# Expert 0's tokens in a fused attention and two-MoE kernel: rows fetched beside the last chunk, the last chunk's own tokens placed by a 0/1 matrix

## The chip, the core and the metric

The kernel runs on one core of a Trainium2 chip. TensorE (PE) multiplies matrices, VectorE (DVE) and ScalarE (ACT) work elementwise on its results, GpSimd (POOL) works elementwise between tiles in SBUF and issues indirect DMAs, SyncE (SP) issues the other DMAs. Every engine works through its own queue in order. The metric is the time of one execution in microseconds, the median of several runs; beside it stands one execution taken with the profiler.

## The reference

What is computed, cut to what matters here:

```python
def _moe2_ref(x, w_gate, w1, w2):           # x: 2176 tokens x 512
    logits = x @ w_gate                      # 8 experts
    order = np.argsort(-logits.flatten())    # best (token, expert) pairs first
    assigned = -np.ones(N); counts = np.zeros(E)
    for idx in order:
        tok, e = idx // E, idx % E
        if assigned[tok] >= 0 or counts[e] >= cap:   # cap = 2176 / 8 = 272
            continue
        assigned[tok] = e; counts[e] += 1
    for e in range(E):
        mask = assigned == e
        out[mask] = np.maximum(x[mask] @ w1[e], 0.0) @ w2[e]

def reference(...):
    x = attention(q_l, k_l, v_l, q_g, k_g, v_g)      # local windows and global rows
    x = (relu(x @ w_in) + alpha * min(x @ w_in, 0)) @ w_out     # d_ff = 2048
    return _moe2_ref(x, w_gate, w1, w2)              # d_ff = 1024 per expert
```

Every expert ends with exactly 272 tokens, in an order of its own that depends on the data.

## The kernel before

Matrices are multiplied in two halves: a number is split into a high half (fp32r, made by ScalarE's cast) and a low half (the rest, by `split`, lines 70 to 73), and a product is the sum of high by high, low by high and high by low, three matmuls. Tokens go in 8 chunks of 272 (`CH`), columns of d_model in four quarters of 128 (`KD`).

The first MoE's second product for all chunks is done at the end of its stage, by `gemm2b` (L1178): for a chunk, 8 blocks `f` of the hidden size by four quarters by 3 are 96 matmuls (L1195), their weights the second half of `w_out`. Two quarters at a time accumulate in two PSUM banks (pool `pH` for the first two quarters, `p4` for the others), and VectorE adds them to the partial result `xo` (L1200). After a chunk its rows are turned by transposes (`rows`, L247), copied by ScalarE, and written to `x2d` in DRAM, one row per token; 16 leftover tokens of seven chunks are collected and written together (`tails`). These steps wait in a list `post` and are done among the next chunk's matmuls. The last chunk's own rows are turned by `last_blocks` (L267) and written by `last_out`.

Meanwhile a router (`phase`, `listing`) finds the experts one after the other on VectorE, with small matmuls on TensorE (counts `pc` L907, column sums `pa` L919, positions `pq`, lists `pl`, `ps`). Its generator is advanced by `advance(x)`, by as many microseconds of TensorE's planned work as the main loop has yielded. TensorE's order is the order in which the code is written (`manual_schedule`), so its router matmuls wait in its queue for VectorE, with the main matmuls behind them. The other engines' order is set by a scheduler from its own estimates.

After the last chunk, `fetch_x(0)` gathers the rows of expert 0's 272 tokens from `x2d` with three indirect DMAs of GpSimd (L1018), `gather(0)` turns them (L1054) and splits them into `xsh` and `xsl`, and `slot(k)` does an expert: `up` 8 x 12 matmuls (L1068), `down` 4 x 24 (L1084). The gather can start only when all rows of `x2d` are written, since an expert's tokens may lie anywhere. While TensorE has nothing else to do it runs 36 matmuls of ones (`busy`, tile `idle`, L108). The weights of expert k+1 come in 8 tiles of 128x1024 (`fetch_1`, `fetch_2`): a DMA into one of three raw buffers, ScalarE's cast, GpSimd's low half, 2.4 us of GpSimd each. PSUM pools have one bank (`px`, tag `tx`) or two (`pH`, `p4`, `pm`).

## Time and profile before

| | us |
|---|---|
| median of 3 runs (840.07 to 842.46) | 841.01 |
| the profiled execution | 843.68 |
| its span, first to last instruction | 841.7 |
| TensorE busy in it | 808.9 (96%) |
| VectorE, ScalarE, GpSimd busy | 473.6, 389.0, 347.9 |
| granted TensorE clock, mean | 0.989 |

Times in rows are microseconds from the span's start. Attention and the first MoE fill 0 to 475, the last products of the first MoE 475 to 591, the eight experts 604 to 832. A row of the timeline gives start, duration, engine, line, operation, out<-in and the number of instructions that it merges; of merged matmuls the duration holds the drain of the last. A bracket gives the idle time of the engine before the row and what ended it, as far as the trace shows; where "issue" or an engine long done is named, it was a wait that the trace doesn't show, often a DMA.

### The profile page before, as it was taken

What the parts mean: (1) busy time and instruction counts of PE and PEld (TensorE: products, weight loads), DVE (VectorE), ACT (ScalarE), POOL (GpSimd) and SP (SyncE); (2) the same over time, 40 slices, a digit from 0 to 9 for tenths busy, and PEclk for the clock granted to TensorE, in tenths of its full rate; (3) what the DMA queues carried; (4) which work ended last, traced back from release to release, by engine and by line L of the source; (5) the groups of instructions that cost most, each with busy time, mean ns of one, the idle gap of its engine ahead of it and who ended that gap; (6) DMA issues with size and microseconds to landing.
All of it is one profiled execution on the core that took longest, in us unless ns stands there. A gap on an engine that the chain in (4) does not pass through costs nothing.

```text
span 841.7 us, 21041 instructions
## 1 busy us (share of the span) xinstructions
PE 808.9 (96%) x8380; PEld 745.1 (89%) x8380; DVE 473.6 (56%) x1672; ACT 389.0 (46%) x970; POOL 347.9 (41%) x299
## 2 busy tenths in 40 slices
PE   6989999999998999999999999999899999999995
PEld 4767878888998999999898999999599999989995
DVE  5888975454389742254343257776577777652120
ACT  5785656465445643433232334341355545454421
POOL 1123413020136532320000365762499978779601
PEclk9989999999999999999999999999999999999998
DMA  9974733631145412011221216434266665656201
GB/s 343 380 287 125 276 120 108 225 129 49 33 167 179 139 52 81 21 60 55 76 84 55 80 53 193 139 77 138 81 219 209 202 194 162 188 164 202 102 26 38
DMA packets 47993, 115.99 MB, mean 138 GB/s; under 512 B 4183, under 2 KB 20951, under 8 KB 45847
## 3 DMA queue, kind: packets, MB, share of 16 engines
q1 hardware_dynamic: 44999, 105.73, 38.8%
q0 software_dynamic: 2896, 8.92, 3.1%
q8 instruction: 66, 1.08, 0.5%
q14 instruction: 32, 0.26, 0.1%
HBM read 96.80 MB, written 17.83 MB: 136 GB/s over the span
## 4 chain that ended last, share of the span: by engine, by line
PE 53%; issue 7%; POOL 4%; DVE 3%; DMA 2%; ACT 1%; POOLq 0%; DVEq 0%
PE h L192 16%; PE h L1195 12%; PE h L1084 7%; PE h L1068 6%; PE y L226 5%; POOL m L73 3%; PE lp L284 2%; DMA raw<-in_moe_w_dram 2%; PE pc L907 1%; PE xt L1054 1%; PE idle L108 1%; PE wp L142 1%; PE yt L247 1%; POOL xg L1018 1%; POOL out_dram L1118 1%
## 5 line engine op out<-in xcount | busy, mean ns | idle before, releaser
L192 PE MATMUL h<-xh,win 128*128 128x272 f32 x768 | 164.7, 300 | 2.9 <-ACT win L72 1.1
L73 POOL TENSOR_TENSOR m<-raw,m 128x1024 fp32r<-128x1024 f32 x64 | 152.1, 2401 | 12.8 <-ACT m L72 10.5
L192 PEld LDWEIGHTS h<-xh,win 128*128 128x128 f32 x768 | 126.7, 192 | 12.5 <-issue 5.0
L192 PE MATMUL h<-xl,win 128*128 128x272 f32 x384 | 112.5, 294 | 1.8 <-DVE xl L73 1.8
L73 POOL TENSOR_TENSOR glo<-g,ghi 128x272 fp32r<-128x272 f32 x64 | 54.6, 859 | 141.2 <-ACT ghi L72 139.6
L226 PE MATMUL y<-ghi,wout 128*128 128x272 f32 x512 | 109.2, 298 | 1.5 <-ACT wout L72 1.5
L1195 PE MATMUL h<-gr,wout 128*128 128x272 f32 x768 | 108.5, 294 | 0.0
L1068 PE MATMUL h<-xsh,m 128*128 128x272 f32 x512 | 105.0, 295 | 0.3 <-ACT xsh L72 0.3
L1084 PE MATMUL h<-hh,m 128*128 128x272 f32 x512 | 103.9, 294 | 0.0
L73 POOL TENSOR_TENSOR gr<-gb,gr 128x272 fp32r<-128x272 f32 x64 | 48.1, 783 | 131.2 <-ACT gr L72 130.7
L1195 PEld LDWEIGHTS h<-gr,wout 128*128 128x128 f32 x768 | 99.4, 189 | 0.5 <-ACT gr L72 0.4
L226 PEld LDWEIGHTS y<-ghi,wout 128*128 128x128 f32 x512 | 82.9, 188 | 6.8 <-issue 3.6
L197 ACT ACTIVATE neg<-h 128x272 f32<-128x272 f32 x128 | 49.9, 395 | 83.3 <-PE h L192 82.3
L1068 PEld LDWEIGHTS h<-xsh,m 128*128 128x128 f32 x512 | 82.1, 188 | 0.5 <-ACT xsh L72 0.5
L1084 PEld LDWEIGHTS h<-hh,m 128*128 128x128 f32 x512 | 81.6, 188 | 0.0
L72 ACT CAST m<-raw 128x1024 fp32r<-128x1024 f32 x64 | 65.5, 1048 | 34.8 <-DMA raw<-in_moe_w_dram 34.8
L192 PEld LDWEIGHTS h<-xl,win 128*128 128x128 f32 x384 | 73.6, 192 | 2.5 <-DVE xl L73 2.5
L1084 PE MATMUL h<-hl,m 128*128 128x272 f32 x256 | 75.2, 294 | 0.0
L1068 PE MATMUL h<-xsl,m 128*128 128x272 f32 x256 | 74.6, 291 | 0.0
L226 PE MATMUL y<-glo,wout 128*128 128x272 f32 x256 | 73.4, 290 | 1.0 <-POOL glo L73 1.0
L198 DVE SCALAR_TENSOR_TENSOR gb<-neg,al,h 128x272 f32<-128x272 f32 x64 | 31.5, 494 | 70.0 <-ACT neg L197 64.8
L400 ACT ACTIVATE pr<-sc,mx 128x128 f32<-128x128 f32 x128 | 49.9, 392 | 31.8 <-DVE mx L398 31.8
(233 smaller groups left out, 1522.8 us busy)
## 6 DMA issues: line engine op xcount, KB each, us to landing
raw<-in_moe_w_dram SPq DMA_DIRECT2D x64, 512.0 KB, 3.7
vv<-in_v_dram SPq DMA_DIRECT2D x16, 1024.0 KB, 8.4
qk<-in_qk_dram SPq DMA_DIRECT2D x14, 720.0 KB, 8.5
raw<-in_moe_w_in_dram SPq DMA_DIRECT2D x16, 512.0 KB, 4.7
raw<-in_moe_w_out_dram SPq DMA_DIRECT2D x16, 512.0 KB, 3.6
xs<-xb SPq DMA_DIRECT2D x16, 272.0 KB, 8.7
xpart<-xd SPq DMA_DIRECT2D x32, 136.0 KB, 2.5
xb<-xs SPq DMA_DIRECT2D x8, 544.0 KB, 3.9
```

Of the source, the lines that this page charges most:

```text
L72: a = A.copy(hi, src)
L73: return a, (lo_eng or V).tensor_tensor(lo, src, hi.bitcast(F32), op=OP.subtract)
L108: T.matmul(ps, x, x.unsqueeze(1).to_broadcast([128, 4, 128]), start=True, stop=True)
L192: T.matmul(ps, wi[:, w, k, fs], x[:, k], start=i == 0, stop=i == 3 * KD - 1)
L197: A.activation(out=neg, in_=ps, func=AF.Relu, scale=-1.0)
L198: epi[0] = V.scalar_tensor_tensor(g, neg, al1[:, hf * KH + f:hf * KH + f + 1], ps, op0=OP.mult, op1=OP.add)
L226: T.matmul(ps, wo[:, w, f, ds_], x[:, f], start=f == 0 and i == 0, stop=f == KH - 1 and i == 2)
L284: T.matmul(lp[r:r + 32], w, x, start=n < 4, stop=n >= LT - 4)
L400: A.activation(out=d["pr", j][:, ii], in_=sc, func=AF.Exp, bias=d["mx", j][:, ii:ii + 1], scale=-1.0, accum_out=d["sm", j][:, ii:ii + 1])
L1068: T.matmul(ps, d["w1"][:, w, kk, fs], x[:, kk], start=i == 0, stop=i == 3 * KD - 1)
L1084: T.matmul(ps, d["w2"][:, w, f, ms], x[:, f], start=i == 0, stop=i == 3 * K3 - 1)
L1195: T.matmul(ps[j], wo[:, w, f, ds_], x, start=f == 0 and a == 0, stop=f == KH - 1 and a == 2)
```

## The change

For the last chunk `gemm2b` is replaced by `last`. It takes the quarters one after the other, each in one bank of `p4` (before: the first two side by side in `pH`). After each quarter `turn` transposes its three token blocks, ScalarE copies them for the write to `x2d`, and they are split (`yh`/`yl` or `yhl`), the low half on GpSimd for the first three quarters. Expert 0's list is clipped (`IDE`): a token of the last chunk is replaced by row 1904, the last chunk's first row, which is written as zeros early on and overwritten only after the fetch. So `fetch_x(0)` needs only the other chunks' rows and is issued during the last chunk; `others` transposes what it brought and copies it to `xe`. The last chunk's own tokens are placed by a matmul: `late_oh`, a 0/1 matrix of 272 tokens by 272 slots, made by VectorE (`late_lists`) right after expert 0's list, from positions that three small DMAs have moved to the chunk's rows (`late_slots`). `take` does the 6 matmuls of a quarter (three token blocks, high and low half), VectorE adds `xe`, ScalarE makes the high and GpSimd (for the last quarter VectorE) the low half.

Expert 0's `up` starts with two blocks at once in `p4`: the 12 products that need only the high halves of the first three quarters, then their 6 with the low half, then the last quarter. The fillers (`busy`) are gone. Cut to what the steps need:

```diff
+        def late_slots(pos):
+            V.tensor_scalar(late_at, pos[:, c14:], -1.0, None, op0=OP.add)
+            V.memset(late_pos, -1.0)
+            nc.sync.dma_start(out=late_pos[:128 - OFF, :2], in_=late_at[OFF:, :2])
...
+        def late_lists():
+            V.tensor_scalar(IDE, IDS[:, 0], float(NTOK - CH), None, op0=OP.min)
+            for b in range(NL):
+                for q, (a, e) in enumerate(blk):
+                    V.tensor_scalar(late_oh[0][:, b, a:e], fr[:, :e - a], late_pos[:, b:b + 1], float(-a),
+                                    op0=OP.subtract, op1=OP.is_equal)
...
         def fetch_x(k):
-            xg = sl.tile([128, 3, DM], F32, name="xg")
+            ids = IDS[:, k] if k else IDE
+            xg = sx.tile([128, 3, DM], F32, name="xg")
             for q, (a, b) in enumerate(SEG):
-                st = P.indirect_dma_start(out=xg[:b - a, q], out_offset=None, in_=x2d,
-                                          in_offset=bass.IndirectOffsetOnAxis(ap=IDS[:b - a, k, q:q + 1], axis=0))
+                P.indirect_dma_start(out=xg[:b - a, q], out_offset=None, in_=x2d if k else x2d[:NTOK - CH + 1],
+                                     in_offset=bass.IndirectOffsetOnAxis(ap=ids[:b - a, q:q + 1], axis=0))
...
+            if k == 0:
+                yield from up(k, (0, 1), range(KD - 1), (0, 2))
+                yield from up(k, (0, 1), range(KD - 1), (1,))
+                yield from up(k, (0, 1), (KD - 1,))
+                f = 2
...
+        def last():
...
+            def turn(d):
+                t = px.tile([128, NL, 128], F32, name="yt", tag="tx")
+                for b, a in enumerate((0, 128, CH - 128)):
+                    T.transpose(t[:, b], xo[:, d, a:a + 128], ident)
...
+                r = gx2.tile([128, NL, 128], F32, name="yr", tag="yr", bufs=3)
+                if d < KD - 1:
+                    A.copy(r, t)
+                    split(*hl, r, lo_eng=P)
+                else:
+                    split(*hl, t)
+                    A.copy(r, t)
...
+            def others(q):
...
+                t = pH.tile([128, KD, 128], F32, name="xt", tag="h1")
+                for d in range(KD):
+                    T.transpose(t[:, d, :n], SLOT[0]["xg"][:n, q, d * 128:(d + 1) * 128], ident[:n, :n])
+                A.copy(SLOT[0]["e"][:, :, a:b], t[:, :, :n])
...
+            def take(d):
+                t = pH.tile([128, CAP], F32, name="xt", tag="h1")
+                for i, hl in enumerate(rows_hl[d]):
+                    for b in range(NL):
+                        T.matmul(t, hl[:, b], late_oh[0][:, b], start=i == 0 and b == 0, stop=i == 1 and b == NL - 1)
+                xh, xl = SLOT[0]["x"]
+                x = SLOT[0]["e"][:, d]
+                V.tensor_tensor(x, t, x, op=OP.add)
+                SLOT[0]["cast"] = split(xh[:, d], xl[:, d], x, lo_eng=P if d < KD - 1 else V)[0]
...
+                    if d == 0 and f and post:
+                        post.pop(0)()
+                        yield 0.4
+                        if not post:
+                            fetch_x(0)
+                    if d and f == 3:
+                        turn(d - 1)
+                        yield 0.4
+                    if d == KD - 1 and f > 4:
+                        others(f - 5)
+                        yield 0.4
+                V.tensor_tensor(xo[:, d], ps, xo[:, d], op=OP.add)
+            for d in range(KD):
+                take(d)
+                if d == 0:
+                    turn(KD - 1)
...
-        st = fetch_x(0)
-        idle = p4.tile([128, 4, 128], F32, name="idle", tag="h4")
-        for _ in range(NB0):
-            busy(idle, ones, 2)
-            advance(0.43)
-        for x in gather(0):
-            busy(idle, ones, 4)
-            advance(x + 0.9)
```

TensorE's order at the end of the last chunk, before (`h` is a main product, `yt` the chunk's own rows turned, `idle` the fillers; behind these rows come more fillers, router counts, the 12 transposes `xt` and then expert 0's first product):

```order
L1195 MATMUL h_8369<-gr,wout 128x272 x15
L267 MATMUL yt<-ident,pt 128x128 x6
L267 MATMUL yt<-ident,pt 16x128 x3
L1195 MATMUL h_8369<-gr,wout 128x272 x9
L267 MATMUL yt<-ident,pt 128x128 x2
L267 MATMUL yt<-ident,pt 16x128
L108 LDWEIGHTS ones
L108 MATMUL idle<-ones 128x512
```

The same place after, from the last three main products on (`xt<-late_oh` is a placement, `h<-xsh` and `h<-xsl` expert 0's products with the high and the low half, `pa` a router sum):

```order
L1289 MATMUL h_8475<-gr,wout 128x272 x3
L1270 MATMUL xt<-ident,xg 128x16 x4
L1277 MATMUL xt<-late_oh,yhl 128x272 x6
L1243 MATMUL yt<-ident,pt 128x128 x3
L1277 MATMUL xt<-late_oh,yh 128x272 x3
L1277 MATMUL xt<-late_oh,yl 128x272 x3
L1277 MATMUL xt<-late_oh,yhl 128x272 x12
L1080 MATMUL h_8666<-xsh,m_7550 128x272 x3
L928 LDWEIGHTS ones
L928 MATMUL pa<-sat_5380,ones 128x8
L1080 MATMUL h_8666<-xsh,m_7550 128x272 x3
L1080 MATMUL h_8684<-xsh,m_7550 128x272 x6
```

The fillers and the wait for fetched rows are replaced by 24 placements, 4 short transposes and 3 of the last quarter.

VectorE's order where expert 0's list `IDS` is finished, before (`gs` is the comparison that a count needs, `lack` and `sat` make the input of the sum that follows, `pt` are the two additions of a chunk):

```order
L863 TENSOR_REDUCE IDS<-pk 128x3
L873 TENSOR_TENSOR gs_5419<-home,th 128x17x31
L938 SCALAR_TENSOR_TENSOR alive<-home,nf,alive 128x8
L916 TENSOR_TENSOR home<-home,th 128x1
L910 TENSOR_TENSOR lack<-pc,rp 31x8
L912 SCALAR_TENSOR_TENSOR sat_5381<-pc,lack 31x8
L1200 TENSOR_TENSOR pt<-h_7522,pt 128x272
L1200 TENSOR_TENSOR pt<-h_7523,pt 128x272
```

and after:

```order
L832 TENSOR_SCALAR late_oh<-fr,late_pos 128x128 x2
L832 TENSOR_SCALAR late_oh<-fr,late_pos 128x16
L882 TENSOR_TENSOR gs_5419<-home,th 128x17x31
L947 SCALAR_TENSOR_TENSOR alive<-home,nf,alive 128x8
L829 TENSOR_SCALAR IDE<-IDS 128x3
L832 TENSOR_SCALAR late_oh<-fr,late_pos 128x128 x2
L832 TENSOR_SCALAR late_oh<-fr,late_pos 128x16
L832 TENSOR_SCALAR late_oh<-fr,late_pos 128x128 x2
L832 TENSOR_SCALAR late_oh<-fr,late_pos 128x16
L925 TENSOR_TENSOR home<-home,th 128x1
L919 TENSOR_TENSOR lack<-pc,rp 31x8
L1217 TENSOR_TENSOR pt<-h_7537,pt 128x272
```

Three of the new instructions stand ahead of `gs`, seven between `gs` and `lack`, and the two additions now stand ahead of `sat`.

GpSimd's order behind the last low halves `gr` of the first MoE, before (`m` are expert 1's weights):

```order
L73 TENSOR_TENSOR gr<-gb_5443,gr 128x272 x2
L1018 DMA xg<-x2d,IDS 128x512 x2
L1018 DMA xg<-x2d,IDS 16x512
L1018 DMA xg<-x2d,IDS 128x512 x2
L1018 DMA xg<-x2d,IDS 16x512
L73 TENSOR_TENSOR m_8604<-raw_8605,m_8604 128x1024
```

and after:

```order
L73 TENSOR_TENSOR gr<-gb_5443,gr 128x272 x2
L1028 DMA xg<-x2d,IDE 128x512 x2
L1028 DMA xg<-x2d,IDE 16x512
L73 TENSOR_TENSOR yhl<-yr,yhl 128x384
L73 TENSOR_TENSOR yl<-yr,yh 128x384
L73 TENSOR_TENSOR yhl<-yr,yhl 128x384
L73 TENSOR_TENSOR xsl<-xe,xsh 128x272 x3
L1028 DMA xg<-x2d,IDS 128x512 x2
L1028 DMA xg<-x2d,IDS 16x512
L73 TENSOR_TENSOR m_8626<-raw_8627,m_8626 128x1024
```

Six low halves stand between the fetch for expert 0 and the fetch for expert 1, and ahead of expert 1's weights.

## Rows read from the trace of the kernel before

**Rows 1.** The page: TensorE busy tenths in 40 slices of the span.

```profile
PE   6989999999998999999999999999899999999995
```

**Rows 2.** TensorE timeline: start us, us, engine, line, operation, out<-in, count.

```profile
575.06 2.39 PE L1195 MATMUL h<-gr,wout 128*128 128x272 f32 x17
...
577.29 0.60 PE L247 MATMUL yt<-ident,pt 128*128 128x128 f32 x4
...
588.60 1.15 PE L267 MATMUL yt<-ident,pt 128*128 128x128 f32 x9
...
589.50 1.38 PE L1195 MATMUL h<-gr,wout 128*128 128x272 f32 x9
...
604.24 0.37 PE L1068 MATMUL h<-xsh,m 128*128 128x272 f32 x1
```

**Rows 3.** Timeline of the other engines there; in brackets idle time before.

```profile
575.73 0.43 DVE L1200 TENSOR_TENSOR pt<-h,pt 128x272 f32<-128x272 f32 x1
...
577.92 0.59 ACT L249 COPY yr<-yt 128x512 f32<-128x512 f32 x1 [0.93 <-PE yt L247]
...
596.25 1.16 POOL L1018 DMA_INDIRECT xg<-x2d,IDS  x1 [22.31 <-DVE alive L938]
```

**Rows 4.** DMA views: issues (median landing), SP timeline, tenths in slices of 583:592.

```profile
xg<-x2d,IDS POOLq DMA_INDIRECT x9, 3.7
...
584.11 0.95 SPq L259 DMA_DIRECT2D x2d<-yr  x1
...
DMA  0000030000016524244332000000000000000000
```

**Rows 5.** Timelines of VectorE, TensorE, GpSimd at expert 0 list, 537:546.

```profile
538.53 0.71 DVE L873 TENSOR_TENSOR gs<-home,th 128x527 bf16<-128x527 f32 x1
...
540.36 0.79 DVE L1200 TENSOR_TENSOR pt<-h,pt 128x272 f32<-128x272 f32 x2
...
537.81 1.87 PE L1195 MATMUL h<-gr,wout 128*128 128x272 f32 x13
...
539.53 0.38 PE L907 MATMUL pc<-ohs,gs 128*128 128x16 bf16 x9
...
541.24 0.18 PE L919 MATMUL pa<-sat,ones 128*128 128x8 bf16 x1
...
541.99 3.91 POOL L73 TENSOR_TENSOR gr<-gb,gr 128x272 fp32r<-128x272 f32 x5 [5.78 <-ACT gr L72]
```

**Rows 6.** Timelines of VectorE and GpSimd, 364:376, tiles of whole numbers.

```profile
368.28 0.30 DVE L709 TENSOR_SCALAR late<-fr,ipf 128x128 bf16<-128x128 int32 x1
...
368.71 1.16 DVE L736 TENSOR_SCALAR fr_b<-fr 128x128 int32<-128x128 int32 x1
...
370.11 0.48 DVE L740 TENSOR_SCALAR spread<-fr_b,pq_f 128x128 bf16<-128x128 int32 x1
...
368.70 1.09 POOL L787 MEMSET gs<- 128x1152 bf16 x1
```

**Rows 7.** Groups of 440:841 by form: count, busy us, mean ns, idle before.

```profile
L73 POOL TENSOR_TENSOR gr<-gb,gr 128x272 fp32r<-128x272 f32 x64 | 48.1, 783 | 131.2 <-ACT gr L72 130.7
...
L1200 DVE TENSOR_TENSOR pt<-h,pt 128x272 f32<-128x272 f32 x32 | 13.4, 435 | 6.6 <-PE h L1195 5.3 <-issue 1.1
```

**Rows 8.** Timelines of GpSimd and TensorE: expert 1's weights and first matmul.

```profile
606.87 16.81 POOL L73 TENSOR_TENSOR m<-raw,m 128x1024 fp32r<-128x1024 f32 x7
...
633.75 0.39 PE L1068 MATMUL h<-xsh,m 128*128 128x272 f32 x1 [0.27 <-ACT xsh L72]
```

**Rows 9.** Windows (busy PE, PEld, DVE, ACT, POOL; clock) and TensorE timeline.

```profile
56.00:60.00 4.00, 3.98 (x28) 3.25 (x28) 2.71 (x9) 3.86 (x14) 1.27 (x1) 0.50 1.01 402
...
596.00:600.00 4.00, 1.40 (x16) 0.65 (x14) 1.06 (x7) 0.00 (x0) 2.97 (x3) 1.00 0.37 85
...
63.38 0.43 PE L192 MATMUL h<-xl,win 128*128 128x272 f32 x1
...
64.06 0.43 PE L192 MATMUL h<-xl,win 128*128 128x272 f32 x1
```

More of the change, by code (lines that the diff above doesn't have):

```diff
@@ L104, in decode @@
         return whole(decoding(pool, src, n))
-    def busy(ps, x, n):
-        for _ in range(n):
-            T.matmul(ps, x, x.unsqueeze(1).to_broadcast([128, 4, 128]), start=True, stop=True)
     WI, WO = {}, {}
@@ L1061, in up @@
             hh, hl = d["h"]
[L1062 to L1073 removed]
+            for f in fs:
+                if ("ps", f) not in d:
+                    pool, tag = (p4, "h4") if f % 2 or (k == 0 and f == 0) else (pH, "h1")
+                    d["ps", f] = pool.tile([128, CAP], F32, name="h3", tag=tag)
+                ps = d["ps", f]
+                for kk in kks:
+                    for i, w, x in ((0, 0, xh), (1, 0, xl), (2, 1, xh)):
+                        if i in terms:
+                            T.matmul(ps, d["w1"][:, w, kk, f * 128:(f + 1) * 128], x[:, kk],
+                                     start=kk == 0 and i == 0, stop=kk == KD - 1 and i == 2)
+                            if kk < KD - 1 or i < 2:
+                                yield 0.113
+                if kks[-1] == KD - 1:
+                    A.activation(out=hh[:, f], in_=ps, func=AF.Relu)
+                    V.scalar_tensor_tensor(hl[:, f], ps, 0.0, hh[:, f].bitcast(F32), op0=OP.max, op1=OP.subtract)
+                    yield 0.113
         def down(k, m):
@@ L1163, in tile_attention_moe_moe @@
         HB = {}
-        NB0 = 12
         SLK, SLK2 = 1.0, 1.0
@@ L1184, in gemm2b @@
             wo = WO[1]
-            end = c == NCH - 1
             if "x" not in tail:
@@ L1229, in tile_attention_moe_moe @@
+        sx = mo.enter_context(tc.tile_pool(name="sx", bufs=1))
         with tc.tile_pool(name="gb_", bufs=1) as gb_:
+            late_oh.append(gb_.tile([128, NL, CH], F32R, name="late_oh"))
+            zero = gx2.tile([128, DM], F32, name="yr", bufs=3)
+            V.memset(zero[:1], 0.0)
+            nc.sync.dma_start(out=x2d[NTOK - CH:NTOK - CH + 1], in_=zero[:1])
             NR = 14
@@ L1236, in tile_attention_moe_moe @@
             for j, c in enumerate(DEF):
-                for x in gemm2b(c):
-                    if x is not None and (j or not post):
+                if j == NDEF - 1:
+                    while listed[0] < 1:
+                        force()
+                for x in gemm2b(c) if j < NDEF - 1 else last():
+                    if j or not post:
                         advance(x)
```

110 lines of the change are left out of this document (53 added, 57 removed).

## The prediction

> **What bounds the kernel now.** I read the page's slices first: TensorE is at nine tenths or more in nearly all of them [rows 1], so a change pays only where TensorE stands still or does work that isn't the kernel's. Then TensorE's timeline around the place of the change [rows 2]. The last of the main matmuls (L1195) starts about 590.6 and TensorE is free at 590.8; expert 0's first matmul (L1068) starts at 604.24. In the 13.4 us between, TensorE does only 3 + 12 transposes, some routing counts and 36 filler matmuls. The rows of the other engines say what the time is [rows 3]: the last chunk's rows are copied and written, the fetch of expert 0's rows starts at 596.25 (it waits for that write), 3.7 us pass until a fetch lands [rows 4], then come transposes and splitting. It is a chain of latencies in which no engine is full. From 604 on TensorE is full again (the slices to the last [rows 1]), so what is saved ahead of 604.24 reaches the end, if nothing else is late.
>
> **The sum** is made against the profiled execution (843.68 us, span 841.7, 2 us around it). The median of the runs shown, 841.01, lies 2.7 us lower; I take the change off the median.
>
> **1. Removed: the chain from the last chunk to expert 0.** -13.4 us, from 590.8 to 604.24 [rows 2]. What has to be done there now comes back in 2 and 3.
>
> **2. Added inside the last chunk.** Its 96 main matmuls stay (0.126 us each: 17 in 2.39 us with 0.25 us of drain [rows 2]). Three waits are new. The chunk now accumulates in the bank pair that the chunk before has just filled, and so waits for VectorE's addition, which starts at 575.73 and takes 0.43 [rows 3], until 576.2; TensorE is free at 575.7: 0.5 us. Its second group of row transposes follows the first after 3 matmuls (12 in before) and shares one bank with it: four transposes take 0.60 us with their drain (577.29 [rows 2]), the copy 0.59 [rows 3], against 0.4 us of matmuls and 0.35 of the transposes themselves: 0.6 us. The third: 0.1. Nine transposes of the chunk itself move, none is added (9 take 0.9 us: 588.60 to 589.50 [rows 2]); 8 of fetched rows are added: 0.8. A count of the router (9 matmuls, 0.38 us with the drain, 0.3 without [rows 5]) falls here that stood in the gap. Together **+2.3** (bounds 1.5 and 3.5).
>
> What hides the fetch: it waits for the write of the 112 tail rows. In before that is issued at 584.11 and its bytes move until about 588.0 (the slices of the DMA view are 0.225 us) [rows 4], 4 us. In the new order the write is issued near 581, so fetches start near 585.1, 1.2 us apart and land 3.7 us later: 588.8, 590.1, 591.4. TensorE reaches their transposes near 591.3, 592.0 and 593.1. Cost nothing, with 1.7 to 2.5 us of cover.
>
> **3. Added behind the last chunk**, which now ends near 593.1. Four short transposes 0.35, three of the last quarter 0.3, 24 placing matmuls by 0.126: 3.0. GpSimd's three low halves of 128x384 (0.78 for 272 columns [rows 7], so 1.1) are done near 584, 588 and 592.4, before they are wanted. The fourth placement waits for a bank that VectorE's additions free (0.435 each [rows 7], one behind the other after the fourth quarter's low half): 0.4. Expert 0's first products need only ScalarE's copies; GpSimd's low halves come at 596.5, 597.7, 598.5, and the 12 high products cover them until 598.7. **+4.05**: the first of them starts near 597.2 (bounds 3.4 and 6.5).
>
> **4. Expert 0's start.** One pair of router steps that ran in the gap (a count, a column sum) now runs among its matmuls: 0.4; ScalarE first casts three weight tiles that landed long ago, as in before, so the first Relu is 0.1 late. **+0.5** (0 and 3; the 3 is a rival below).
>
> **5. The 0/1 matrix.** Nine VectorE instructions (six of 128x128, three of 128x16) and a clip of the list enter the router's chain near 538.5. TensorE works in order, and its next count waits for VectorE. In before the comparison ends at 539.24 and TensorE's count starts at 539.53, right behind 13 matmuls; so there is some 0.2 us of slack [rows 5]. Three of the instructions stand ahead of that comparison, six and the clip behind it, and now both additions stand ahead of the test that the column sum at 541.24 waits for. Nearest price: the comparison of the same tile with a per-row scalar, 0.30 us [rows 6]; independent instructions overlap on VectorE by about 0.1 (two additions of 0.435 take 0.79 [rows 5]), so 0.2 to 0.25 each. First wait 0.4, second 1.0: **+1.4** (0.9 if they run as the fastest of their size, 2.6 at 0.48, the price of a second 128x128 comparison). All main matmuls stand queued behind those two waits, so this is on the path. A row speaks of much worse: an integer operation on the same 128x128 tile takes 1.16 us beside GpSimd's memset of 1.09 [rows 6]. At 538 GpSimd is idle: 5.78 us of idleness end at 541.99 [rows 5]. I take the quiet price.
>
> The Trainium skill (GPSIMD Engine Reference, 8. Key points) says that GpSimd and VectorE share their SBUF interfaces and contend when VectorE runs a two-port mode or has two SBUF inputs. By that rule the lists cost the high price only beside a busy GpSimd; the 1.16 us row agrees, and at that price the sum is the rival "lists" below, 843.8 where the quiet price gives 836.0.
>
> **Sum:** -13.4 + 2.3 + 4.05 + 0.5 + 1.4 = -5.15; I take **-5.0**: 838.7 for a profiled execution and **836.0** for the median. With all terms at their good ends it is -7.6 (833.4). Smaller edits at nothing: a zero row written near 370 (1x512), three tiny transfers of slots that land 10 us before their use, the split of the x2d writes by quarters (each behind work of TensorE).
>
> **Rivals.**
> *The weights set the pace.* GpSimd makes expert 1's low halves (2.4 us a tile) on raw tiles whose three buffers it must free itself; ScalarE's casts wait for these loads, and Relus and splits queue behind the casts. In before GpSimd starts on them at 606.87, 2.6 us behind expert 0, and expert 1's first matmul, at 633.75, already waits 0.27 us for ScalarE's last split [rows 8]. Now GpSimd must first make expert 0's low halves and fetch expert 1's rows (3.6 us) after the last write has landed near 598.9: 602.5, plus term 5: 603.9. It is then 5 us behind expert 0. If this chain sets the end, the gain is 606.87 - 603.9 = 3.0: 838.0. Against it: in the new order one cast fewer stands ahead of each split of expert 1. 12%.
> *The fetch isn't hidden.* Its GpSimd instruction waits for every write to x2d so far, and one that lands late moves all three. Beyond 2 us it costs one to one, with the chunk's last 15 matmuls queued behind: 4.5 us late gives 838.5. 9%.
> *The lists at the high price (slower side).* One place, 538 to 543: six instructions by 1.16 and three by some 0.8 are 9.4 us instead of the 1.6 assumed, hence 7.8 us more wait of TensorE: 843.8. From 0.9 us each on the change is lost. For: same tile, same engine; against: GpSimd's idleness there. 8%.
> *The clock.* Without the fillers TensorE may fall to its lower level. In before it was granted 1.00 with only 1.40 us of work in 596 to 600 [rows 9], and the largest new wait is 0.6, which speaks against it. At 0.50 (56 to 60) three matmuls of 272 columns take 0.68 us (the first starts at 63.38, the fourth at 64.06), 0.1 more each [rows 9]; a stretch of 10 us at that level loses some 4.4: 840.4. 5%.
> The Trainium skill (TensorE: Matmul & The Clock Gate, What's actually happening) has the clock halved after idleness, which is what the fillers guard against; the 596 to 600 row shows no fall.
> *Better:* lists nearly free, fewer waits in 2 and 3: 833.5. 10%.
>
> **How the numbers follow.** Forecast 56%, between 834 and 838.4. A difference of 0.3% (2.5 us) is about what a measurement of this kernel can tell from none: 838.5 and 843.5 are the bounds. Faster: 56 + 10 + 10 of the weights + 3 of the fetch = 79%. Same: 2 + 6 + 5 = 13%. Slower: 8%. The range 833.2 to 840.2 leaves out the lists at the high price, most of the clock and the tail of "better".
>
> **What would show it.** Right: first matmul of expert 0 some 6 us earlier (near 598.6), 4 to 5 us behind the last chunk's last one; two TensorE waits of 0.4 and 1 us near 539 to 543 ended by VectorE; fetches landed before TensorE asks; granted clock 1.00. Wrong: a TensorE wait of over 1 us ended by a DMA or GpSimd between 575 and 600; list instructions above 0.5 us; a growing gap to expert 1 near 627 ended by ScalarE.

## The result and the profile after

| | before | after |
|---|---|---|
| median, us (6 runs each) | 842.39 | 835.42 |
| ratio after/before | | 0.9916 (95%: 0.9894 to 0.9937) |
| profiled execution, us | 843.68 | 836.83 |
| its span, us | 841.7 | 835.1 |

The change gains 7.0 us by the medians (5.3 to 8.9 by the interval); 5.0 were forecast, at 836.0, taken off the 841.01 that the first three runs of the kernel before had given. In two later sets the changed kernel ran again beside the one before: 833.46 against 841.50 and 834.07 against 843.02, both at 0.9893 (0.9874 to 0.9912, and 0.9870 to 0.9917): 8 to 9 us. So direction and range hold, and the gain was forecast too small.

The page's slices of the changed kernel (TensorE's busy tenths, its granted clock) show no dent in the 29th slice (585 to 605 us), where the kernel before had one [rows 1]:

```profile
PE   6989999999999999999999999999999999999995
PEclk9989999999999999999999999999999999999999
```

The answer to [rows 2], TensorE's timeline at the start of the last chunk (the two waits for a bank) and at its end (start, us, engine, line, operation, count, idle time before):

```profile
575.61 1.02 PE L1289 MATMUL h<-gr,wout 128*128 128x272 f32 x6 [0.28 <-DVE pt L1217]
...
577.75 0.66 PE L243 MATMUL yt<-ident,pt 128*128 128x128 f32 x4 [0.30 <-ACT yr L245]
...
592.06 0.62 PE L1289 MATMUL h<-gr,wout 128*128 128x272 f32 x3
592.61 0.42 PE L1270 MATMUL xt<-ident,xg 16*128 16x16 f32 x4
592.96 1.02 PE L1277 MATMUL xt<-late_oh,yhl 128*128 128x272 f32 x6
...
595.96 0.99 PE L1277 MATMUL xt<-late_oh,yhl 128*128 128x272 f32 x6 [0.16 <-DVE xe L1280]
596.78 0.54 PE L1080 MATMUL h<-xsh,m 128*128 128x272 f32 x3
```

The last fetched rows (L1270) are transposed without a wait, placing starts, and expert 0's first product comes at 596.78 in place of 604.24, 4.4 us behind the last main product (592.4). GpSimd there, the answer to [rows 3] and [rows 8]:

```profile
585.62 1.16 POOL L1028 DMA_INDIRECT xg<-x2d,IDE  x1 [12.73 <-DVE home L999]
...
589.23 1.02 POOL L73 TENSOR_TENSOR yhl<-yr,yhl 128x384 fp32r<-128x384 f32 x1
...
602.39 7.08 POOL L73 TENSOR_TENSOR m<-raw,m 128x1024 fp32r<-128x1024 f32 x3
```

The fetches start at 585.62, near the 585.1 that was worked out. The bracket names VectorE; that they wait for the write of the tail rows, issued 5.15 us earlier at 580.47, is inferred. The low halves don't start near 582 to 591 one by one: they stand in GpSimd's queue behind the fetches and run from 589.23 to 592.16 in a row, 0.8 us ahead of the first placement. Expert 1's weights start at 602.39, 5.6 us behind expert 0's first product (forecast 5).

The answer to [rows 5], VectorE and TensorE at expert 0's list:

```profile
537.00 0.62 DVE L832 TENSOR_SCALAR late_oh<-fr,late_pos 128x128 fp32r<-128x128 int32 x3
...
538.34 1.15 DVE L832 TENSOR_SCALAR late_oh<-fr,late_pos 128x128 fp32r<-128x128 int32 x6
...
539.78 0.79 DVE L1217 TENSOR_TENSOR pt<-h,pt 128x272 f32<-128x272 f32 x2
540.49 0.14 DVE L921 SCALAR_TENSOR_TENSOR sat<-pc,lack 31x8 bf16<-31x8 f32 x1
...
540.69 0.18 PE L928 MATMUL pa<-sat,ones 128*128 128x8 bf16 x1 [0.54 <-DVE sat L921]
```

Nine list instructions take 1.77 us, some 0.2 each, and both additions now stand ahead of the test (L921) for which TensorE's column sum waits 0.54 us. Of the first wait that was forecast (0.4, at the count) 0.13 us is there, too short for a bracket.

**Stretches.** To compare executions I cut the span at four starts on TensorE: the first product of the gated rows (G), the last main product of the last chunk (M), expert 0's first product (U), and its first product of the second matrix (D). All runs of this study:

| kernel | G at | G to M | M to U | U to D | D to end | G to end |
|---|---|---|---|---|---|---|
| before | 476.6 | 114.0 | 13.6 | 14.1 | 223.4 | 365.1 |
| before_again | 473.2 | 114.0 | 15.1 | 14.1 | 224.8 | 368.0 |
| after | 475.0 | 117.4 | 4.4 | 15.2 | 223.1 | 360.1 |
| again | 473.7 | 117.4 | 4.4 | 15.1 | 222.1 | 359.1 |
| again_2 | 473.2 | 117.8 | 4.4 | 15.0 | 221.1 | 358.3 |
| e1, no fillers (before) | 472.4 | 114.0 | 12.7 | 17.7 | 222.7 | 367.1 |
| e2, lists twice | 474.3 | 120.7 | 4.4 | 15.0 | 222.8 | 362.8 |
| e3, lists on GpSimd | 479.2 | 117.2 | 4.4 | 15.0 | 221.9 | 358.5 |
| e5, lows on VectorE | 472.7 | 117.9 | 4.3 | 15.3 | 221.8 | 359.3 |
| e6, plain order | 477.8 | 117.4 | 4.4 | 15.8 | 222.7 | 360.3 |
| e7, fetch late | 473.0 | 125.4 | 6.6 | 15.6 | 221.2 | 368.8 |
| e8, placing half again | 472.7 | 117.4 | 5.5 | 15.4 | 221.4 | 359.8 |
| e9, lists, clip, bank | 473.6 | 115.9 | 4.4 | 15.1 | 221.3 | 356.6 |
| e10, e9 and two edits | 475.8 | 115.4 | 4.4 | 13.9 | 223.7 | 357.3 |

### The profile page after: what moved, and what is told of

Its sections match the earlier page's. It is cut to its first block, busy times and chain, and to the rows that moved or that the text cites. A ratio compares the mean times of both kernels' runs of the same rounds, so it can differ in the third digit from the quotient of the medians.

```text
span 835.1 us, 21073 instructions
## 1 busy us (share of the span) xinstructions
PE 802.2 (96%) x8368; PEld 742.8 (89%) x8368; DVE 475.4 (57%) x1687; ACT 393.3 (47%) x980; POOL 353.3 (42%) x305
## 4 chain that ended last, share of the span: by engine, by line
PE 51%; issue 6%; POOL 4%; DVE 3%; DMA 3%; ACT 1%; POOLq 0%; SPq 0%; DVEq 0%; ACTq 0%
PE h L188 16%; PE h L1212 10%; PE h L1080 7%; PE y L222 5%; PE h L1098 5%; POOL m L73 3%; DMA raw<-in_moe_w_dram 3%; PE lp L265 2%; PE h L1289 1%; PE pc L916 1%; PE yt L243 1%; PE wp L138 1%; POOL out_dram L1132 1%; POOL xg L1028 1%; ACT m L72 1%
## 5 line engine op out<-in xcount | busy, mean ns | idle before, releaser
L1080 PE MATMUL h<-xsh,m 128*128 128x272 f32 x512 | 103.2, 293 | 0.2 <-DVE hl L1086 0.2
L1212 PE MATMUL h<-gr,wout 128*128 128x272 f32 x672 | 95.0, 294 | 0.0
L1212 PEld LDWEIGHTS h<-gr,wout 128*128 128x128 f32 x672 | 87.0, 189 | 0.4 <-ACT gr L72 0.4
```

The costliest lines, as they stand in the source:

```text
L1080: T.matmul(ps, d["w1"][:, w, kk, f * 128:(f + 1) * 128], x[:, kk], start=kk == 0 and i == 0, stop=kk == KD - 1 and i == 2)
L1212: T.matmul(ps[j], wo[:, w, f, ds_], x, start=f == 0 and a == 0, stop=f == KH - 1 and a == 2)
```

## Experiments

### The same two kernels again

> The changed kernel once more. In the two traces shown, the stretch from the first product of the gated rows (start 476.6 before, 475.0 after) to the end of the span went from 365.1 to 360.1 us, -5.0, which is what was forecast, but the medians lie 7.0 apart, and 1.6 us of the span's -6.6 stand ahead of 476, where the change has no instruction on TensorE's path. Theory: that 1.6 us is chance (arrival of the first data, length of the stretch at the lower clock near 55 to 66 us); then the first product of the gated rows starts anywhere between 474.5 and 477 here, the stretch behind it is again 360.1 within 0.4, and the medians come nearer to -5. Rival: something ahead is really shorter; then it starts at 475.0 again and the medians stay near -7.

> The kernel before once more, for a second trace. Theory (the start of the first gated product is chance, the stretch behind it a property of the kernel): the product starts anywhere between 472 and 479.5, as in the traces so far of both kernels, and from it to the end of the span it is 365.1 us within 0.7, against 360.1 and 359.0 in the two traces of the changed kernel. Rival (the 1.6 us ahead of 476 belong to the change): it starts at 476.6 again.

> The changed kernel beside the version above on the same chip. Theory: 359.0 to 360.1 us from the first gated product to the end of the span, 3.5 to 4.5 more than the version above, and a median 3 to 5 us above it; first gated product anywhere between 472 and 479.5.

Measured: times above; the kernel before 843.07 us (its reference runs 843.02). G starts at 473.7, 473.2 and 473.2, and over all traces anywhere from 472.4 to 479.2, in both kernels: the 1.6 us ahead of G in the first pair are chance. But behind G neither kernel is as constant as I held: 365.1 and 368.0 before, mean 366.6, against 359.1 (358.3 to 360.1) for the changed kernel: 7.5 us, which agrees with the medians. So what I expected of the three repeats came true only for G: the second trace of the changed kernel took 1.0 us less from G to end than the first, and its median lay 8.0 us below the kernel before, not nearer 5; the third was 1.0 us above e10 in G to end and 0.9 below it in the median, where 3 to 5 more were expected. By the means the difference is +3.5 in G to M, -10.0 in M to U, +1.0 in U to D, and -2.0 in D to end, a stretch to which the prediction gave nothing. The means are of two traces before and three after.

Two things vary between the traces of the kernel before. First its chain, M to U. TensorE waits 2.49 us for the fetched rows in before_again and 2.60 in the trace of [rows 2]; the fetches take as long (596.49 is 9.3 us behind M, 600.00 there is 9.4), but in before_again the clock falls behind the wait. TensorE's wait in the trace of [rows 2], then the timeline of before_again and its windows (us, busy, granted clock, DMA):

```profile
600.00 0.63 PE L1054 MATMUL xt<-ident,xg 128*128 128x128 f32 x4 [2.60 <-issue]
```

```profile
596.49 0.63 PE L1054 MATMUL xt<-ident,xg 128*128 128x128 f32 x4 [2.49 <-issue]
...
598.87 1.91 PE L108 MATMUL idle<-ones 128*128 128x512 bf16 x4
...
596.00:598.00 2.00, 1.51 (x10) 0.93 0.50 148
598.00:600.00 2.00, 2.00 (x9) 0.50 0.00 0
600.00:602.00 2.00, 2.00 (x10) 0.72 0.00 0
602.00:604.00 2.00, 2.00 (x24) 1.00 0.33 86
```

At 0.50 (1.2 GHz) four fillers take 1.91 us instead of the 1.03 of the first trace, where the same windows stand at 1.00: the chain is 15.1 us instead of 13.6, with all its fillers. Second, expert 1's start. ScalarE and TensorE in before_again, then in again:

```profile
631.85 1.04 ACT L72 CAST m<-raw 128x1024 fp32r<-128x1024 f32 x1 [1.74 <-DMA raw<-in_moe_w_dram]
632.80 0.20 ACT L72 CAST xsh<-xt 128x64 fp32r<-128x64 f32 x1
...
633.06 0.39 PE L1068 MATMUL h<-xsh,m 128*128 128x272 f32 x1 [1.57 <-ACT xsh L72]
```

```profile
622.78 1.05 ACT L72 CAST m<-raw 128x1024 fp32r<-128x1024 f32 x1 [1.06 <-DMA raw<-in_moe_w_dram]
623.73 0.20 ACT L72 CAST xsh<-xt 128x64 fp32r<-128x64 f32 x1
...
624.71 0.29 PE L1080 MATMUL h<-xsh,m 128*128 128x272 f32 x1
```

In both, the last split of expert 1's rows (128x64) stands on ScalarE behind a weight cast that waits for its tile. In the kernel before, that makes TensorE wait 0.27 [rows 8] or 1.57 us. Counted from expert 0's own splits, twelve weight casts stand ahead of it in the kernel before, ten in the changed one; there the split is done 0.8 us before it is wanted, and from D to expert 1's first product it takes 14.1 to 14.8 us where it took 15.4 and 16.6. That the two casts fewer are the reason is argued, not shown: no run moved them alone, and in e1 below, which has the twelve, the split is done 1.67 us before it is wanted and the stretch takes 14.8.

### The fillers taken out of the kernel before

```diff
         for _ in range(NB0):
-            busy(idle, ones, 2)
             advance(0.43)
         for x in gather(0):
-            busy(idle, ones, 4)
             advance(x + 0.9)
```

> The kernel before with its 36 filler matmuls left out (the router's steps stay where they were). Theory: the chain between the last chunk and expert 0 is latency on other engines, and the clock doesn't fall: the first product of expert 0 still comes 13.6 us behind the last main product (13.3 to 13.7), the granted clock stays 1.00 from 590 to 640, and the time is that of the kernel before within 0.3%. Rival (the clock): a level of 0.50 for some 10 us behind 600, 4.4 us more. Rival (fillers in the way): the transposes of the fetched rows queue behind fillers and come earlier without them, 0.5 to 1 us less. For the question ahead of 476: as the kernel before, its first gated product should start at 476.6 if the start is a property of the kernel, anywhere if it is chance.

Measured: 842.93 us, ratio 1.0022 (1.0004 to 1.0040). Windows of TensorE and the others (busy us of PE, PEld, DVE, ACT, POOL; granted clock; DMA), and TensorE's timeline:

```profile
588.00:592.00 4.00, 0.41 (x9) 0.32 (x9) 3.52 (x14) 0.65 (x2) 0.00 (x0) 0.82 0.40 139
592.00:596.00 4.00, 0.28 (x2) 0.31 (x3) 0.00 (x0) 0.00 (x0) 2.98 (x3) 0.50 0.39 100
...
600.00:604.00 4.00, 3.73 (x16) 3.61 (x17) 2.53 (x10) 2.23 (x3) 3.38 (x3) 0.50 0.46 139
...
590.62 0.41 PE L907 MATMUL pc<-ohs,gs 128*128 128x16 bf16 x9 [2.88 <-DVE gs L873]
595.72 1.09 PE L1054 MATMUL xt<-ident,xg 128*128 128x128 f32 x4 [4.69 <-DMA xg<-x2d,IDS]
```

Both rivals are right at once. Without fillers TensorE waits 2.88 and 4.69 us, the granted clock falls to 0.50 until 604, and expert 0's first half takes 3.6 us longer (17.7); 1.3 of that stand in two waits for VectorE (0.63 and 0.68 us), the rest goes with the clock. The fillers also stood in the way: M to U is 1.0 shorter than in the first trace. So by the times they were worth little in the kernel before (0.04 to 0.40%), and G to end, 367.1, lies between the two traces with fillers. [rows 9] (1.00 in 596 to 600) was one execution with fillers on either side; it said little of a gap without them. In the changed kernel nothing is lost without them: its longest wait between 536 and 620 is 0.72 us in the first trace and 0.65 in the two others, and the clock there is 1.00 in all three.

### The 0/1 matrix: twice, and on GpSimd

```diff
                 with tc.issue_after(st.ins):
                     late_lists()
+                    late_lists()
```

> The changed kernel with the 0/1 matrix (and the clip of the list) made twice, one behind the other, on VectorE: ten instructions more in the router's chain at expert 0's list. Theory (the lists lie on the path, since TensorE's next column sum stands behind them and all main products behind that): about 0.2 us each, so 1.5 to 2.1 us more, all of it as TensorE's wait for VectorE near 540, where the changed kernel waits 0.54; the stretch from the first gated product to the last main product grows from 117.4 to about 119.2. Rival (the lists fit into idle time of VectorE and what was lost there is something else): under 0.4 us more. Rival (the high price beside a busy GpSimd): 6 us or more.

Measured: 836.65 us; G to M 120.7, 3.3 more than in the first trace of the changed kernel, between the theory's 2.1 and the rival's 6.

```profile
541.75 0.19 PE L929 MATMUL pa<-sat,ones 128*128 128x8 bf16 x1 [2.37 <-DVE sat L922]
...
542.00:544.00 2.00, 2.00 (x10) 0.50 0.04 8
544.00:546.00 2.00, 2.00 (x14) 0.74 0.00 0
546.00:548.00 2.00, 2.00 (x19) 1.00 0.00 0
```

The wait grows by 1.83 us, within the theory's 1.5 to 2.1, so the lists lie on the path at about 0.2 us each. The other 1.4 us go with the clock: behind this one wait of 2.37 us it is at 0.50 in the next window (10 matmuls in 2 us; 19, some of them short, in the window at 1.00).

```diff
-                    V.tensor_scalar(late_oh[0][:, b, a:e], fr[:, :e - a], late_pos[:, b:b + 1], float(-a),
+                    P.tensor_scalar(late_oh[0][:, b, a:e], fr[:, :e - a], late_pos[:, b:b + 1], float(-a),
```

> The changed kernel with the nine instructions of the 0/1 matrix on GpSimd, which is idle for 5.8 us there; VectorE keeps the clip. Theory: TensorE's wait near 540 falls from 0.54 to at most 0.1 and the column sum comes 0.6 to 0.9 us earlier; the stretch from the first gated product to the last main product shrinks from 117.4 to about 116.6, and 0.5 to 0.9 us of it reach the end. Rival (shared access): while GpSimd writes the matrix, VectorE's additions and comparisons there get slower, and nothing is gained. Rival (GpSimd's own queue): the nine instructions (some 0.5 us each, 4 to 5 us) hold up the low halves of the gated rows behind them, and TensorE waits for one of these later: 0 to 2 us lost.

Measured: 835.85 us (0.9919, 0.9898 to 0.9939); G to M 117.2, and the wait is still there, 0.65 us.

```profile
541.18 0.71 DVE L882 TENSOR_TENSOR gs<-home,th 128x527 bf16<-128x527 f32 x1
...
541.94 2.25 DVE L829 TENSOR_SCALAR IDE<-IDS 128x3 int32<-128x3 int32 x1
...
539.00 5.15 POOL L73 TENSOR_TENSOR gr<-gb,gr 128x272 fp32r<-128x272 f32 x7
```

GpSimd now makes the matrix from 533 to 539 (with one low half among it) and then seven low halves without a pause until 544.15, and beside them the clip of 128x3, 0.16 us in the changed kernel, takes 2.25 on VectorE and ends with the last of them. The comparison ahead of it, of two tensors, keeps its 0.71 beside the same GpSimd. The Trainium skill (GPSIMD Engine Reference, 8. Key points), as the prediction cites it, has an operation with two SBUF inputs contend as well; the measurement decides, and it shows no contention for this one. So a high price beside a busy GpSimd exists, for the clip; in the changed kernel GpSimd was idle there (534.9 to 540.7), as the prediction had worked out. The nine instructions themselves were never run on VectorE beside a busy GpSimd. The Trainium skill (VectorE: DVE Perf Modes, Mode 2×_2P) says that an operation of one tensor and a scalar in SBUF can take both read ports, and an operation of two tensors cannot; that fits which of the two was held up, but no run here shows the mode.

```diff
-            V.tensor_scalar(IDE, IDS[:, 0], float(NTOK - CH), None, op0=OP.min)
+            P.tensor_scalar(IDE, IDS[:, 0], float(NTOK - CH), None, op0=OP.min)
...
-                ps = p4.tile([128, CH], F32, name="h2", tag="h4")
+                ps = (p4 if d else pH).tile([128, CH], F32, name="h2", tag="h4" if d else "h1")
```

(and the matrix on GpSimd as above)

> The changed kernel with the 0/1 matrix and also the clip of the list on GpSimd, and with the last chunk's first quarter in a bank of the other pair, which is free. Theory on the lists: with the matrix alone on GpSimd the wait near 540 stayed (0.65 us), because the clip, 0.16 us in the changed kernel, took 2.25 beside the now busy GpSimd; with the clip away too, VectorE stands there as in the kernel before, the wait is gone, and from the first gated product to the end of the chunk before the last it takes 1.0 us less. Theory on the bank: TensorE's wait of 0.28 us for VectorE's addition goes, 0.3 to 0.5 us less. Together the stretch from the first gated product to the last main product shrinks from 117.4 to 116.0, and the time by 1.0 to 1.5. Rivals: the wait was not the lists' (stays near 0.5); the additions and comparisons themselves get slower beside the busy GpSimd (the wait stays, with longer instructions of VectorE than in the changed kernel); the gain is given back at expert 1's weights (stretch from the first product of expert 0 to the end, 238.3 and 237.2 in the two traces, grows by as much).

Measured: 832.60 us, ratio 0.9895 (0.9876 to 0.9914). G to M is 115.9, 1.5 less than in the changed kernel, as expected: 1.0 up to the end of the chunk before the last (its last product starts 99.08 us behind G, in the changed kernel 100.04, in the kernel before 99.05), so that is what the lists cost, and 0.6 at the bank. The bracket there says 0.28: it counts from the end of the matmul before, drain included, while the next one stands 0.52 us behind where it would follow without a wait (five products from 574.46 at 0.126 us each reach 575.09, the next starts at 575.61). A short wait of TensorE costs about twice its bracket here. Three waits of TensorE are left between 530 and 605:

```profile
574.86 0.66 PE L243 MATMUL yt<-ident,pt 128*128 128x128 f32 x4 [0.30 <-ACT yr L245]
593.07 0.99 PE L1277 MATMUL xt<-late_oh,yhl 128*128 128x272 f32 x6 [0.16 <-DVE xe L1280]
599.89 0.39 PE L1080 MATMUL h<-xsh,m 128*128 128x272 f32 x1 [0.74 <-DVE hl L1086]
```

It has the shortest G to end of all (356.6), and the lowest median of all kernels here; the times alone don't tell it from the changed kernel (833.46 and 834.07 in the other sets).

### The fetch issued late

```diff
                         yield 0.4
-                        if not post:
-                            fetch_x(0)
                     if d and f == 3:
                         turn(d - 1)
+                        if d == KD - 1:
+                            fetch_x(0)
                         yield 0.4
```

> The changed kernel with GpSimd's three fetches of expert 0's rows issued behind the three low halves of the last chunk's rows instead of ahead of them. The third low half can start when its copy is done, near 590.5; so the fetches start near 591.5 instead of 585.6, 5.9 us late, and land near 595.1, 596.4 and 597.7. Theory (hidden with little cover): TensorE asks at 590.6, 591.4 and 592.6; where the fetches are on time the cover is 0.7 to 1.4 us, so 4.5 to 5.2 us of waits ended by the DMA of xg stand inside the last chunk, and the stretch from its last main product to expert 0's first one stays 4.4 to 4.8. Rival (some 3 us of cover or more): under 3 us. Rival (the clock falls in the wait, as it did without the fillers): the granted clock drops to 0.50 for some microseconds behind, and 2 to 4 us come on top.

In this version the row of zeros has been overwritten by the time it is fetched, so what stands under the chunk's own tokens isn't zero, and expert 0's results aren't the reference's. Measured: 844.70 us, ratio 1.0030 (1.0016 to 1.0045): slower than the kernel before.

```profile
591.42 1.16 POOL L1028 DMA_INDIRECT xg<-x2d,IDE  x1 [1.30 <-DMA x2d<-yr]
...
595.06 1.11 PE L1270 MATMUL xt<-ident,xg 128*128 128x128 f32 x4 [6.32 <-DMA xg<-x2d,IDE]
...
590.00:592.00 2.00, 0.00 (x0) 0.69 0.01 1
592.00:594.00 2.00, 0.00 (x0) 0.50 0.29 66
```

Counted from the last chunk's first product (573.61 here, 575.61 in the changed kernel), the first fetch starts 17.8 us behind it instead of 10.0: 7.8 later, for a wait of 6.3. It is 7.8 and not the 5.9 expected because the third low half also waits for ScalarE's cast behind the copy (0.5 us) and the fetch for a write of the chunk's own rows (1.30 us idle, in the bracket). So the cover was 1.5 us (1.7 to 2.5 in the prediction, 0.7 to 1.4 before this run), and the theory of little cover holds. The rival of the clock holds too: it stands at 0.50 from 592 to 604, M to U is 6.6 instead of 4.4 to 4.8, and G to end is 9.7 above the changed kernel's mean, 3.4 more than the wait. The hidden fetch is what the gain hangs on: late, it costs more than the change gains, and a fetch that isn't hidden costs more than its own time.

### GpSimd's low halves, and the high products first

```diff
-                    split(*hl, r, lo_eng=P)
+                    split(*hl, r)
...
-                SLOT[0]["cast"] = split(xh[:, d], xl[:, d], x, lo_eng=P if d < KD - 1 else V)[0]
+                SLOT[0]["cast"] = split(xh[:, d], xl[:, d], x, lo_eng=V)[0]
```

> The changed kernel with the six low halves that GpSimd makes for expert 0 (three of 128x384, three of 128x272) on VectorE; the order of the products is kept. Theory (GpSimd's part is worth what VectorE has no room for): the additions of the placements and the low halves alternate on VectorE, so the fourth placement waits about 0.8 instead of 0.16 us for its bank, and the three wider ones (0.6 each) stand in the router's chain: 1.2 us more (0.4 to 2.5), as TensorE's waits for VectorE between 580 and 600. Rival (GpSimd's part is free either way): 0 within 0.3. Rival (GpSimd freed starts on expert 1's weights earlier than 5.6 us behind expert 0's first product, and that is worth more): faster.

Measured: 834.58 us (0.9921, 0.9897 to 0.9946); G to end 359.3, as the changed kernel's mean. My theory falls: the fourth placement doesn't wait at all, and one count waits 0.28. TensorE's wait behind the first Relu is 1.16 us here (0.22 to 0.65 in the changed kernel's traces), but U to D is 15.3, as long as there within 0.3. VectorE makes the wide low half in about half of GpSimd's 1.02 us and has room for it:

```profile
589.97 0.55 DVE L73 TENSOR_TENSOR yhl<-yr,yhl 128x384 fp32r<-128x384 f32 x1
```

That GpSimd makes them is worth nothing here that one trace and four runs can show.

```diff
             if k == 0:
-                yield from up(k, (0, 1), range(KD - 1), (0, 2))
-                yield from up(k, (0, 1), range(KD - 1), (1,))
-                yield from up(k, (0, 1), (KD - 1,))
-                f = 2
```

> The changed kernel with expert 0's first products in the order of the other experts: bank by bank, high, low and high of each 128 columns in turn, instead of the high products of both banks first. Theory: the fourth low half is done 2.7 us behind the first product of expert 0 (599.49 and 596.78 in the trace of the changed kernel); in the plain order the product that needs it is the eleventh, 1.2 us behind the first, so TensorE waits 1.2 to 1.5 us once, ended by VectorE, and maybe 0.2 for GpSimd before; 1.1 to 1.5 us more in the stretch from expert 0's first product to its first product of the second matrix (15.2 in the changed kernel). Rival (the order is worth nothing, the low halves come in time): 0 within 0.2.

Measured: 836.08 us (0.9917, 0.9896 to 0.9938); U to D 15.8, 0.6 to 0.8 more, with one wait where it was expected, of 0.53 us, not 1.2 to 1.5.

```profile
601.95 0.39 PE L1080 MATMUL h<-xsl,m 128*128 128x272 f32 x1 [0.53 <-DVE xsl L73]
...
601.47 0.43 DVE L73 TENSOR_TENSOR xsl<-xe,xsh 128x272 fp32r<-128x272 f32 x1
```

The mechanism holds, at half the size: the low half is done 2.3 us behind expert 0's first product (599.62), not 2.7 (in the changed kernel's trace too it is 2.3: 599.06, not the 599.49 that I had read), and the product that needs it, with a column sum ahead of it, is due 1.8 us behind, not 1.2.

### What is ahead of expert 0, and what is behind

```diff
-                for i, hl in enumerate(rows_hl[d]):
+                for j, i in enumerate((0, 0, 1)):
                     for b in range(NL):
-                        T.matmul(t, hl[:, b], late_oh[0][:, b], start=i == 0 and b == 0, stop=i == 1 and b == NL - 1)
+                        T.matmul(t, rows_hl[d][i][:, b], late_oh[0][:, b], start=j < 2 and b == 0, stop=j != 1 and b == NL - 1)
```

> The changed kernel with 12 placing products more behind the last chunk: the products of the high halves are made twice, the first time for nothing, since the sum is begun anew. Theory (TensorE's path sets the end): expert 0's first product comes 5.9 us behind the last main one instead of 4.4, and the whole 1.5 us reach the end: from the first gated product to the end 361.0 instead of 359.5 (mean of 360.1 and 359.0). Rival (the weights set the pace): GpSimd starts on expert 1's weights when the last write of rows has landed and its fetches of expert 1's rows are out, which these products don't move (the last quarter's rows are turned behind the first placement: 0.4 us later at most); then the stretch behind expert 0's first product gets shorter by what is added ahead of it, and the total grows by under 0.5.

Measured: 836.04 us (0.9923, 0.9898 to 0.9948), 2.0 above the changed kernel's median in the same set. Twelve products add 1.1 to M to U (the 0.16 us wait for a bank is gone), U to D grows by 0.3, and D to end is 221.4 (changed kernel: 221.1 to 223.1). G to end is 0.7 above the mean. The trace can't tell theory from rival at this size; the times lean to the theory, but the intervals of the two ratios overlap (0.9898 to 0.9948 and 0.9870 to 0.9917), so it stays open.

```diff
-        with tc.issue_after(SLOT[0]["cast"].ins):
...
-            fetch_1(1)
...
+            if not k and n > 2.75 and 1 not in SLOT:
+                with tc.issue_after(SLOT[0]["relu"].ins):
+                    fetch_1(1)
```

(on top of e9; the chunk before the last also turns its second row group in a bank of `pH`)

> The changed kernel with the matrix and the clip on GpSimd and the first quarter in the other bank pair (as in the run before, 356.6 us from the first gated product to the end), and two edits more: the second row group of the chunk before the last is turned in a bank of the other pair (TensorE waits 0.30 us there for ScalarE's copy), and ScalarE casts expert 1's first three weight tiles (2.94 us) behind expert 0's first two Relus instead of ahead of them (TensorE waits 0.74 us for the low half behind the first Relu). Theory: both waits go, 355.6 us; the time 8.5 to 10 us below the kernel before. Rival (the casts are wanted early): GpSimd starts on the weights later or ScalarE's Relus meet them later, and the stretch behind expert 0's first product grows by as much as was saved: 356.6 or more.

Measured: 834.98 us (0.9897, 0.9870 to 0.9925), against 834.07 of the changed kernel beside it. ScalarE and TensorE:

```profile
598.86 0.73 ACT L1086 ACTIVATE hh<-h 128x272 fp32r<-128x272 f32 x2 [2.23 <-PE h L1081]
599.49 2.93 ACT L72 CAST m<-raw 128x1024 fp32r<-128x1024 f32 x3
...
630.87 0.38 PE L917 MATMUL pc<-ohs,gs 128*128 128x16 bf16 x9 [0.56 <-DVE gs L883]
633.33 0.17 PE L929 MATMUL pa<-sat,ones 128*128 128x8 bf16 x1 [0.71 <-DVE sat L922]
```

The bank edit does what was expected: the wait of 0.30 us is gone and G to M is 0.5 less. The casts stand behind the first two Relus and the wait of 0.74 us is gone: U to D is 13.9, 1.2 less. D to end is 223.7, 2.4 more than in e9. In the sum this is the rival (357.3), and new waits for VectorE of 0.56 and 0.71 us stand in expert 1. That the moved casts cause them isn't shown: in the changed kernel's own three traces D to end spreads over 2.0 us, and waits of 1.00, 0.32 and 0.46 us stand at the same two instructions in two of them.

## Why the prediction came out as it did

Sign, mechanism and range are right: at one place TensorE did nothing of the kernel's own, that place is gone, and nothing new of that size took its place. Counted from G, expert 0's first product comes 5.9 us earlier (some 6 were forecast). The time forecast (836.0) lies 0.6 from the one measured, the gain (5.0) 2.0 to 4 from it; part of that closeness is luck, since the median of the kernel before was 1.4 us higher with six runs than with the three that the forecast was taken from. By its own steps:

- **1 and 3** (-13.4 and +4.05, together -9.35): -9.2 against the trace it was made from (13.6 to 4.4), -10.0 against the mean of two. The 4.05 was right to within 0.3; the 13.4 came from an execution in which the clock survived the chain's wait of 2.60 us, and in the second one it didn't. That is the rival "clock" with the opposite sign: the change takes away a wait behind which the clock could fall. With the rows fetched under the chunk's products, M to U is 4.3 or 4.4 in every run that left this place alone.
- **2** (+2.3): G to M grew by 3.4 to 3.8; less 1.0 for the lists that is 2.4 to 2.8. The bank waits were priced right: their brackets say 0.28 and 0.30 us where 0.5 and 0.6 were put, but taking them out gave 0.56 (e9) and 0.52 (e10). The fetch was hidden with 1.3 to 1.5 us of cover. GpSimd's low halves were put at the wrong times, since the fetches ahead of them hold the queue; that cost nothing.
- **5** (+1.4): 1.0. The first wait is 0.13 us, not 0.4, and the second 0.54, not 1.0; the price of 0.2 each was right. One line of its rival was not: with 1.6 us assumed for nine instructions, a gain of 5.0 is lost at some 0.7 us each, not from 0.9.
- **4** (+0.5): +1.0, so it was put at half its size. TensorE waits 0.22 for the low half behind the first Relu, and 0.72 for a test (L921) that stands on VectorE behind a low half whose Relu stands on ScalarE behind a weight cast:

```profile
610.44 0.18 PE L928 MATMUL pa<-sat,ones 128*128 128x8 bf16 x1 [0.72 <-DVE sat L921]
```

  In e8, e9 and again_2 the first of these is 0.65 to 1.34.
- **The missing term**: D to end, -2.0 by the means (the ranges are 223.4 to 224.8 before and 221.1 to 223.1 after), 1.7 of it between D and expert 1's first product. The rival "weights" had the right place and the wrong sign. GpSimd does start 5.6 us behind expert 0, but I left as a remark that one cast fewer stands ahead of expert 1's splits. That remark was probably a term: TensorE's wait of 0.27 or 1.57 us for the last split is in both traces of the kernel before and in none of the changed one's. It is the least certain of the terms, since e1, the kernel before without fillers, hasn't that wait either (222.7).

With the stretches as measured the sum is 3.5 - 10.0 + 1.0 - 2.0 = -7.5.

Of the other rivals, the fetch was hidden as worked out (e7 shows what it costs where it isn't), and the lists at the high price weren't met, though e3 shows that the price exists for a neighbour. The Trainium skill (TensorE: Matmul & The Clock Gate, What's actually happening) has the clock halved after idleness; e1, e2, e7 and before_again agree: the clock stood at 0.50 there. In the first trace of the kernel before it stayed 1.00 behind an idle stretch of 2.60 us, so that trace, from which I argued that it wouldn't fall, couldn't tell.

## What to carry to other kernels

A wait of TensorE that is taken out is worth its length and what the clock loses behind it in some executions: look at a second trace before pricing a gap by one. A short wait in a bracket can cost twice what it says (0.28 and 0.56 us here), so it is priced by the time between the two products around it. An engine's queue carries waits to places that have nothing to do with them (a cast waiting for its tile ahead of a 0.2 us split, a fetch waiting for a write ahead of low halves), so a reordering is priced by what now stands ahead of each short instruction that TensorE needs. Fillers dropped alone cost this kernel 0.2% (e1); dropped together with the wait that they bridge, they left no fall of the clock behind.

## What the runs showed of the hardware that I hadn't expected

- Length alone didn't decide whether the clock falls: behind waits of 2.37 us (e2) and 2.49 (before_again) it was 0.50 and some 1.5 us were lost beyond the wait, behind 2.60 us (before) it stayed 1.00. Behind 1.34 (e8), 1.47 (e7) and 1.57 us (before_again) it was 1.00.
- A 128x3 clip on VectorE took 2.25 us instead of 0.16 beside a GpSimd that ran without pause (e3).
- Where G starts varies by 6.8 us over all traces here, without order by kernel. Part of it is the clock early on: in the earliest start (e1) and the latest (e3) the windows of TensorE alone (busy, clock, DMA) read, in this order,

```profile
60.00:70.00 10.00, 10.00 (x136) 1.00 0.54 183
```

```profile
60.00:70.00 10.00, 10.00 (x101) 0.65 0.44 165
```

  A single profiled execution of this kernel tells a total only to some microseconds; stretches cut at the same instructions can be compared to a few tenths, except where DMAs or the clock set them (M to U of the kernel before: 13.6 and 15.1; D to end of the changed one: 221.1 to 223.1).
